# Attention into a long-convolution gate: batch 2 crossed by DMA, the last batch's complex sums on VectorE, a new order of all engines

## The chip, the cores and the metric

The kernel runs on one core of one Trainium2 chip. The metric is device time of that core in microseconds, the median of several runs. The engines have their usual names: TensorE (PE, with its weight loads as PEld), VectorE (DVE), ScalarE (ACT), GpSimd (POOL) and SyncE (SP). POOL issues the loads that turn 32-bit inputs into 16-bit ones, SP the other transfers.

## The reference

Two operations follow each other. The first is attention with a bias that falls with distance, 4 batches, 8 heads, 768 positions, 64 columns a head. A query sees the first 8 keys and the 96 latest ones:

```
scores = q @ k^T / sqrt(64) - slope[h] * dist        # dist 96 for the far first keys
a = softmax(scores where (key < 8) or (0 <= query - key < 96))
x = (a @ v), heads side by side                      # [4, 768, 512]
```

The second takes x through a gated convolution over the whole sequence:

```
x1, x2, x3 = split(x @ w_proj)                       # 512 columns each
conv = irfft(rfft(x2) * rfft(filter))                # along the 768 positions
out = (x1 * conv * x3) @ w_out                       # [4, 768, 512], float32
```

## The kernel before, in words

**Stages of a batch.** Attention works on seven tiles of keys: each holds the 8 first keys and 120 further ones, so that one tile of keys and up to 216 queries cover the local window. The tiles form three groups c = 0, 1, 2 (tiles 0 and 1, 2 and 3, 4 to 6). For each pair of heads and each group PE forms the scores (`scores`, L759), ACT takes the exponential (L774), DVE multiplies by a mask that holds bias and window (L791; batch 0 adds the bias on PE instead, L753). For each half of the heads and each group, PE multiplies by the values (`values`, L809 and L814), DVE takes the reciprocal of the sum, and DVE or ACT normalises into `xn` (L833 on DVE as one instruction, L837 on ACT as one small instruction for each slice of 64 columns). PE turns `xn` (`transpose_x`, L854) and a copy puts it into `xT`.

From `xT` PE forms the gates x1 and x3 (`gate`, L932): ACT takes x1 out of PSUM with a scale (L318), and DVE multiplies x3 by it (L946). In the last batch ACT copies x3 too (L942) and DVE multiplies both in SBUF (L944).

The Fourier transform of 768 positions is split by butterflies (`butterfly`, DVE, L868 to L888) before the projection of x2 (`conv`, PE L993, copied into `ab`). Six spectral blocks X come out of one matmul each (`spectra`, L1124, copied into `X`). Blocks 0 and 1, and 2 and 3, are real and imaginary parts. Their complex product with the filter is four real products (DVE, L1142 and L1145 into `pp`) and a difference and a sum (DVE, L1153 and L1154). Blocks 4 and 5 have another form (L1131, L1134). In the last batch, which `SUMPE` names, the difference and the sum are left out: PE adds the four products while it transforms back, with six matmuls for each block of the output instead of four (L1023, L1027, L1030). DVE then joins the parts (`mixed`, L1088 to L1094), forms y (`gated`, L1108 and L1109), multiplies by the gates (L1113), and PE projects y by w_out (L1059). ACT or DVE scales the result into `ot`, and SP stores it (L1070).

**Turning queries and keys.** The scores need queries and keys with the head's columns on the partitions, `QT` and `KT`. There are two ways. Batches 0 to 2 load them by head pairs, turn them on PE with an identity (`turned`, L707, L710), and copy them out of PSUM (one copy for a QT, three or four for a KT). Batch 3, which `TILES` and `CROSS` name, loads them by tiles of positions (`load_tiles`: 6 loads of queries, 7 of keys) and lets SP issue 13 transposing transfers from SBUF to SBUF through the crossbar (`cross`, L406). One such transfer writes 128 columns of all four head pairs in QT or KT. Two small transfers fill the 8 first keys into the other tiles (`kg` below, L392).

`qn` and `kn` (the loaded rows), `QT`, `KT`, `X` and `pp` exist once. So batch 3's loads overwrite the rows of batch 2, and its transposes overwrite the QT and KT of batch 2. The values and the gates have two buffers.

**What sets the order.** Every operation is a node of a graph (`Plan`), numbered as it is made. A long text, ORDER, lists the numbers in the order of issue, each with its engine and, for a group of matmuls, the PSUM banks that it takes: `83P0` is operation 83 on PE into bank 0. A copy out of PSUM may stand on A (ACT) or V (DVE). Each engine runs its own operations in the order of the text, and waits are put in where data demand them. `i1b5` stands for one spare matmul of 512 columns into bank 5, which computes nothing. Since SP's queue is one sequence, a transfer that waits holds all behind it. The same holds for POOL.

The order before puts batch 2's transposes on PE between the last projections and spectra of batch 0, and its scores behind them. Batch 3's crossing stands behind the last of POOL's loads.

Of the kernel before, what the change touches and what calls it, by code (L numbers as in the profile page):

```python
# [17 lines left out]
P = 128  # L18
# [10 lines left out]
def act(n):  # L29
    return 0.06 + n / 1200.0  # L30
# [11 lines left out]
0V 1V 2A 3G 45S 30A 47S 4V 34V 6A 9A 32G 56S 49S 5V i1b5 22P0 55G 23A 54G 7G 24A 10V 17P1 8V 33V 25V 51G 18A  # L42
35G 19A 12P2 13A 46V 52G 37A 48V i2b5 83P0 38A 53G 81P3 72G 20V 26A 61G 63G 21A 14V 44V 50V 15V 39V 201P1 93P2
36V 87P4 84A 202V 57V 60G 43A 82A 207V 95P3 16A 94A 97P67 209V 85P2 65G 64G 29V 11V 62G 88A 41V 91P0 203V 66G
96V 149P45 239G 42A 236G 86V 98A 204A 234G 150A 40V 89P3 121P67 151P45 238G 58V 208V 90V 205V 122A 152A 117P23
92V 99P67 206V 103P45 211V 233G 212V 118A 213V 235G 100A 119P23 101P67 153P01 104A 105P45 120A 102A 154A 27V
214V 115P23 237G 106V 215V 59S 116A 107V 155P67 78A 216V 110P01 111V 128P23 232G 157P45 156A 77A 217V 67G
220P6 112V 162P01 221A 158V 108P6 73A 113P7 129V 130V 123P23 109A 224P6 159V 131P4 114V 79A 222P7 245G 68G
341P5 241G 243G 225A 163V 124V 76A 223A 218P6 31V 240G 164V 125V 337P0 132V 28V 339P1 244G 340V 165P7 126P4
127V 247G 160P2 74A 335P1 338A 137P4 342A 166V 193V 139A 161V 133P7 376P23 219A 242G 336V 246G 354P45 414P01  # L50
377A 138P6 69G 167P2 355A 134P3 415A 183V 135A 184V 351P45 352A 192V 194V 140V 373P01 186V 185V 136V 343P6
374A 459G 169A 248G 195V 172P7 70G 71G 171P4 464G 187V 196V 173A 226P01 347P2 227A 345P3 411P45 251G 344V 252G
353V 349P0 145P6 75A 174V 249S 412A 348V 141P2 346V 254G 357P45 350V 228A 417P01 147A 375V 253G 420P67 188V
168P3 255G 197V 458G 256G 470G 356V 189V 143A 170V 142P2 465G 418A 471G 144V 175P0 358A 146P1 421A 382P67 198V
191V 460G 360P23 177A 413V 199V 148V 80A 190V 383A 379P45 380A 258P0 463G 361A 259A 229P67 416V 200V 378V
271P1 363P45 272A 230A 422V 275P2 461G 364V 273P3 231A 250S 466G 276A 284P6 419V 385P01 362V 274A 384V 286P7
359V 260P2 386V 365V 387V 462G 560P3 287A 479G 478G 285A 469G 261A 368P45 381V 279P0 366P1 472G 561A 473G 369V
468G 277P2 288V 423P67 370V 280A 262P3 289V 264P0 278A 367A 371P1 424V 263A 467G 425V 372A 282V 566P2 428P45
266P1 390P67 257G 265A 706G 567A 562P0 281V 267A 429V 388P3 391V 563A 179P2 430V 564P1 392V 176P4 181A 180P0
565A 389A 269V 576P67 268V 182V 178V 426P1 577A 431P2 393P0 432V 427A 394V 579P45 687G 580A 598P67 639P23 640A  # L60
396P0 698G 572P1 574P4 270V 395P5 298P2 407P3 696G 573A 599A 474G 397A 450V 570P1 568P6 449V 451V 695G 452V
404P5 575A 299A 408P7 694G 409A 403P4 571V 684G 398V 636P23 585P01 453V 410V 690G 569A 283V 454V 405A 600V
637A 582P67 445P4 480G 586A 481G 699S 399P2 447A 406V 433P3 446P4 455V 477G 702G 292P5 583A 435A 401A 456V
457V 645P67 607P01 448V 693G 293A 300P3 638V 646A 290P2 294P5 441P4 295A 304P6 442P5 581V 476S 608A 482G 584V
443A 400P7 475S 578V 302P4 697G 296P0 609V 688G 301A 291A 647V 303A 444V 689G 402V 485P1 604P45 297A 305A 587V
642P23 486A 307V 306V 605A 601P67 641V 691G 643A 685S 483P0 496P1 593P23 602A 308V 594V 603V 497A 484A 498P4
606V 588P67 487P5 589V 683G 701G 499A 595A 437P4 309V 489P0 590V 490A 488A 704G 310V 615P67 439A 692G 644V
311V 703G 610P23 611V 616V 700S 653P01 491P5 617A 438P4 612V 312V 511P2 440V 654V 686S 434P3 313V 596P4 618P6
512A 597A 492A 619A 500P7 655V 591P2 592A 613P5 314V 493V 501A 502P4 509P6 494V 648P01 504P7 656P2 705G 614A
624P5 510A 787S 649V 505A 513V 657A 632P6 503A 436V 315V 620P7 507V 629P4 621P3 626A 323P5 495V 506V 789S 514V  # L70
625P2 650A 508V 785S 634A 622A 651P0 324A 652A 628P6 784S 515P7 786S 517P5 529P1 518A 623V 527P3 627V 316V
675V 523P0 516A 528A 519P2 630A 670P5 525P3 793S 526A 521P7 633P6 530A 520A 791S 332P3 674V 317P2 524A 635V
333A 631V 672A 662P3 522A 803P45 790S 677V 806P67 800P01 318A 664A 801A 788S 676V 326P2 804A 795S 532V 327A
329P3 320P0 678V 330A 321A 796S 707P2 679V 663P3 807A 797P01 531V 680V 794S 825P67 533V 708A 534V 822P45 798A
682V 826A 720P2 666P0 535V 805V 536V 665V 671P3 823A 537V 681V 828P67 673V 721A 819P45 711P1 658P3 668A 820A
712A 799V 792S 829A 724P2 861P01 827V 870P67 660A 867P45 725A 722P3 540V 538V 802V 319S 334S 871A 733P2 868A
539V 723A 709P6 809P45 726P3 541V 734A 808V 554P7 331S 872V 810V 727A 735P3 542P2 830V 811V 862A 863V 555A
710A 814P01 836P45 864P67 736A 815V 543A 824V 837V 667P3 816V 865A 659P2 869V 838A 866V 715P6 713P7 661V
878P01 325S 669V 714A 548P2 728P7 812P3 879V 716A 821V 880V 737V 817P6 831P45 729A 873P01 839P7 322S 832V 730V
818A 813A 874V 551P3 731V 833A 875V 328S 732V 718V 557P6 881P4 738V 834P5 876P0 545P1 840A 835A 882A 877A  # L80
856P7 556S 717V 841P4 904V 741P0 903V 719V 745P5 546A 749P1 558A 742A 843A 549A 746A 857P6 842P0 906V 905V
907V 908V 851P2 858A 909V 750A 753P7 559S 844A 747P5 754A 739P4 743P1 751P0 883P7 744A 912P1 748A 910V 740A
852P4 752A 756V 859A 755V 913A 924P6 853A 936P2 552A 925A 911V 884P5 757V 854A 938P6 914P3 845V 937A 758V
916P2 939A 915A 860V 928P3 759V 888P6 210A 917A 760V 553S 940V 761V 929A 920P4 550S 918P3 886A 919A 926P2 941V
764V 921A 923V 922V 932P3 889P5 927A 898P4 933A 930P3 544S 894P2 885A 946P7 931A 762V 896A 942P3 935V 957P1
846P2 934V 855V 947A 958A 961P7 943A 944P1 962A 948P3 945A 763V 959P0 949A 963P7 960A 964A 765V 951V 950V
847P1 781P0 547S 891A 965V 966V 952V 967V 769P5 899P7 848A 953V 770A 900A 968V 954V 969V 772P2 955V 970V 956V
766P3 849A 773A 971V 850V 974V 774S 901A 972V 893P2 767A 782A 975V 775P7 973V 890A 892V 778P3 771S 895A 897V
982P2 768S 985V 779A 902V 783S 976P3 887V 776A 979P7 986V 983A 987V 993P2 989P6 988V 780S 994P 1001P0 980V
# [1208 lines left out]
```

## Time and profile before

| | |
|---|---|
| median of three runs | 165.75 us (165.38 to 165.85) |
| span of the profiled execution | 163.0 us, first to last instruction |
| instructions | 4256 |
| granted TensorE clock | 0.999 |
| POOL's last load issued | 82.6 to 84.4 us |
| last crossing issued (end of the issue) | 100.8 us |

The profiled execution has no time of its own beside its span. The median of the runs stands 2.75 us above that span, and this difference is taken as what lies around the span. The views give busy times for each engine, a table of stretches of time, groups of instructions by source line and shape, waits by what ended them, and packets by DMA queue (q0 holds what POOL issues, q1 what SP issues). In a group's row stand the line, engine, operation, output and inputs with shapes, the count, then the busy time in us and the mean duration in ns, and the idle time of the engine just before.

### The profile page before, as it was taken

How to read it: one execution, taken by the hardware profiler on the slowest of the kernel's cores; microseconds unless marked ns; L12 is line 12 of the kernel's file. 1: busy time of each engine (PE TensorE's matmuls, PEld its weight loads, DVE VectorE, ACT ScalarE, POOL GpSimd, SP SyncE). 2: the span in 40 equal slices, each digit the busy share in tenths (PEclk: the TensorE clock that was granted, in tenths of full speed). 3: DMA queues.
4: the chain of work that ended last, by engine and by line, in shares of the span. 5: the costliest groups of instructions: out<-in, count | busy, mean ns of one | idle time of the engine just before them, and what ended most of it. 6: DMA issues, size and time to landing. Idle time of an engine off the chain costs nothing.

```text
span 163.0 us, 4256 instructions
## 1 busy us (share of the span) xinstructions
PE 154.0 (94%) x1604; PEld 94.7 (58%) x1604; DVE 151.6 (93%) x356; ACT 150.3 (92%) x327; POOL 76.8 (47%) x101
## 2 busy tenths in 40 slices
PE   6599997999999999999999999999999999999980
PEld 2274355866655777666577584445676664584440
DVE  6599699999999999999999999999999999999960
ACT  8999996999999999999999999999998999997850
POOL 7999199999979997999970000000000000000000
PEclk9999999999999999999999999999999999999999
DMA  5999999999999999999999964630100106000684
GB/s 170 200 166 164 165 150 138 147 158 174 190 162 154 139 136 136 149 153 163 161 129 162 134 121 101 236 150 0 64 4 6 66 0 253 5 4 0 264 332 178
DMA packets 84956, 21.95 MB, mean 135 GB/s; under 512 B 75584, under 2 KB 81992, under 8 KB 84936
## 3 DMA queue, kind: packets, MB, share of 16 engines
q0 software_dynamic: 73040, 12.11, 98.4%
q1 hardware_dynamic: 11896, 9.57, 21.4%
q8 instruction: 12, 0.20, 0.5%
q14 instruction: 8, 0.07, 0.1%
HBM read 25.40 MB, written 6.29 MB: 194 GB/s over the span
## 4 chain that ended last, share of the span: by engine, by line
PE 85%; ACT 9%; DVE 3%; issue 1%
PE bank L932 26%; PE bank L993 13%; PE bank L1059 13%; PE bank L759 7%; PE bank L854 4%; PE bank L809 4%; PE bank L707 3%; PE bank L1023 3%; PE bank L1124 3%; PE bank L814 3%; PE bank L753 2%; ACT E L774 2%; ACT KT L314 1%; PE bank L1030 1%; PE bank L690 1%; ACT QT L314 1%
## 5 line engine op out<-in xcount | busy, mean ns | idle before, releaser
L932 PE MATMUL bank<-xT,w 128*128 128x384 f16 x256 | 48.2, 326 | 0.0
L774 ACT ACTIVATE E<-bank 128x864 f16<-128x864 f32 x48 | 41.0, 911 | 0.3 <-PE bank L759 0.2
L932 PEld LDWEIGHTS <-w 128*128 128x128 f16 x256 | 23.9, 98 | 15.8 <-issue 0.3
L339 POOL DMA_DIRECT2D vn<-in_v_dram x28 | 26.3, 979 | 1.1 <-DMA w<-in_moe_w_proj_dram 1.1
L339 POOL DMA_DIRECT2D kn<-in_k_dram x25 | 21.8, 892 | 5.4 <-DMA vn<-in_v_dram 4.0
L1059 PE MATMUL bank<-wo,y 128*128 128x512 f16 (+1 forms) x100 | 22.6, 371 | 0.0
L339 POOL DMA_DIRECT2D qn<-in_q_dram x25 | 21.8, 885 | 0.1
L791 DVE TENSOR_TENSOR E<-E,mask 128x864 f16<-128x864 f16 x36 | 20.3, 591 | 0.0
L318 ACT ACTIVATE x<-bank 128x384 f16<-128x384 f32 x32 | 16.6, 547 | 0.0
L318 ACT ACTIVATE ot<-bank 128x512 f32<-128x512 f32 (+1 forms) x23 | 13.3, 610 | 3.5 <-PE bank L1059 3.1
L809 PE MATMUL bank<-vn,E 128*128 128x65 f16 x224 | 15.3, 193 | 0.9 <-DVE xn L833 0.7
L993 PE MATMUL bank<-w,xs 128*128 128x512 f16 x64 | 15.9, 379 | 0.0
L809 PEld LDWEIGHTS <-E 128*128 128x128 f16 x224 | 14.0, 97 | 2.3 <-DMA vn<-in_v_dram 0.4
L1059 PEld LDWEIGHTS <-y 128*128 128x128 f16 x100 | 9.5, 98 | 9.9 <-DVE y L1113 0.5
L814 PE MATMUL bank<-vn,E 128*128 128x65 f16 x192 | 15.0, 193 | 0.0
L314 ACT CAST eo<-bank 128x384 f16<-128x384 f32 x32 | 14.3, 513 | 0.6 <-PE bank L1030 0.2
L314 ACT CAST X<-bank 128x512 f16<-128x512 f32 x24 | 14.3, 636 | 0.4
L314 ACT CAST ab<-bank 128x512 f16<-128x512 f32 x24 | 14.3, 629 | 0.4 <-PE bank L993 0.3
L833 DVE TENSOR_TENSOR xn<-bank,rc 128x512 f16<-128x512 f32 (+1 forms) x19 | 14.3, 771 | 0.1
L814 PEld LDWEIGHTS <-E 128*128 128x128 f16 x192 | 13.1, 97 | 1.9 <-issue 1.2
L759 PE MATMUL bank<-QT,KT 64*128 64x216 f16 (+2 forms) x224 | 13.7, 242 | 0.0
L759 PEld LDWEIGHTS <-KT 64*128 64x128 f16 x224 | 7.9, 94 | 8.7 <-issue 6.8
(163 smaller groups left out, 334.1 us busy)
## 6 DMA issues: line engine op xcount, KB each, us to landing
out_dram<-ot SPq DMA_DIRECT2D x23, 256.0 KB
vn<-in_v_dram POOLq DMA_DIRECT2D x28, 120.0 KB, 7.6
kn<-in_k_dram POOLq DMA_DIRECT2D x16, 96.0 KB, 5.1
qn<-in_q_dram POOLq DMA_DIRECT2D x16, 96.0 KB, 5.2
w<-in_moe_w_proj_dram POOLq DMA_DIRECT2D x4, 256.0 KB, 5.8
kn<-in_k_dram POOLq DMA_DIRECT2D x7, 120.0 KB, 6.2
g<-in_moe_filter_fft_dram POOLq DMA_DIRECT2D x1, 768.0 KB, 10.6
qn<-in_q_dram POOLq DMA_DIRECT2D x6, 128.0 KB, 7.0
```

Of the source, the lines that this page charges most:

```text
L314: {"A": nc.scalar.copy, "V": nc.vector.tensor_copy, "G": nc.gpsimd.tensor_copy}[e](out, in_)
L318: self.nc.scalar.mul(out, in_, c)
L339: return self.g.op(eng, 0.57 + 0.00035 * nbytes[0] if eng == "G" else 0.5, lambda _: e.dma_start(dst, src), w=w, r=r, nbytes=nbytes, name= ...
L759: nc.tensor.matmul(bs[hh].f32()[:, off:off + w], self.KT[hs, hp, P * m:P * m + P], self.QT[hs, hp, KL * m:KL * m + w], start=(off == 0 and ...
L774: g.op("A", act(864), lambda _: nc.scalar.activation(eo, bs[0].two()[:, :, 0:432].rearrange("p h (m w) -> p h m w", m=2), Act.Exp, scale=s ...
L791: g.op("V", dve(864, 2), lambda _: nc.vector.tensor_mul(eo, eo, mk), r=[("mask", 2 * hp), ("mask", 2 * hp + 1)], w=[("E", hp, gi)], name=" ...
L809: nc.tensor.matmul(o[:, n, hh], ef[:, at:at + P], vt[:, t, 2 * hp + hh, 0:D + 1], start=first, stop=(t == 0), skip_group_check=True)
L814: nc.tensor.matmul(o[:, n, hh], ef[:, at:at + P], vt[:, t - 1, 2 * hp + hh, 0:D + 1], start=False, stop=True, skip_group_check=True)
L833: nc.vector.tensor_mul(to, o[:, :, :, 0:D], rc.to_broadcast([P, 2, 2 * nt, D]))
L932: nc.tensor.matmul(bk.f32()[:, 0:h], self.w[:, c, o + P * j:o + P * j + P], self.xT[:, c, h * s:h * s + h], start=(c == 0), stop=(c == 3))
L993: nc.tensor.matmul(bk.f32(), src[:, c], w[:, c, DM:2 * DM], start=(c == 0), stop=(c == 3))
L1059: nc.tensor.matmul(bk.f32()[:, 0:n], y[:, c, P * t:P * t + P], self.wo[:, c, cs], start=(c == 0), stop=(c == 3))
```

## The change

- `TILES` and `CROSS` name batch 2 as well: its 16 loads by head pairs become 13 loads by tiles, its 48 transposes on PE and the 16 copies out of PSUM go, and SP issues 13 crossbar transposes and two small copies for it.
- `SUMPE` is empty: in batch 3 DVE forms the difference and the sum (two instructions for each of two pairs of blocks), and PE's inverse has four matmuls for a block instead of six.
- `WHOLE` names batches 0 to 2: the products of blocks 0 to 3 are formed together, in two instructions of 2048 columns instead of four of 1024, and their sums in two of 1024 instead of four of 512. `parts` places them behind all four X.
- ORDER is new throughout. Beside the order it moves some operations between ACT and DVE. Of normalising, ACT gets 8 of 24 (5 before); of the QT copies 1 of 8 (6 of 12); of the KT copies 5 of 8 (7 of 12). Two of the filter's copies and one `ab` go from ACT to DVE. Batch 2's first scores come directly behind the last turning of batch 1's `xn`, and batch 3's scores earlier among the projections of batch 2. The spare matmuls are one at the start and two ahead of the last output projection.
- The further options (`PAIR_T`, `PAIR_AB`, `PAIR_X`, `PAIR_EO`, `PAIR_OT`) join two banks into one copy; all are empty, so their paths aren't taken. `ab` and `ot` become views of one tile each.

```diff
 ORDER = """
-0V 1V 2A 3G 45S 30A 47S 4V 34V 6A 9A 32G 56S 49S 5V i1b5 22P0 55G 23A 54G 7G 24A 10V 17P1 8V 33V 25V 51G 18A
...
-990P 777S 977A 978S 997P7 998P 995A 984S 991A 999A 1002P 1003V 981S 996S 992S 1000S 1004S
+45S 34V 1V 2A 0V i1b2 4V 3G 5V 22P4 23A 47S 8V 56S 11V 49S 32G 53G 46V 6A 17P1 52G 7G 18A 24V 25V 12P0 13A 26A 19V
...
+979P 980A 981S 982P6 983P 984V 985S i2b0 986P4 987P 988V 989S
 """
...
-    SUMPE = (3,)
+    SUMPE = ()
...
+    WHOLE = (0,1,2)
...
-    TILES = (3,)
-    CROSS = (3,)
+    TILES = (2, 3)
+    CROSS = (2, 3)
...
+    def parts(self, b):
+        self.spectra(b, (2, 3))
+        if b in self.WHOLE:
+            self.products(b, (0, 1, 2, 3))
+        self.spectra(b, (4, 5))
...
+    def products(self, b, pair):
+        nc, g, X, DM = self.nc, self.g, self.X, self.DM
+        n, m = pair[0] // 2, len(pair) // 2
+        xs = X[:, pair[0]:pair[0] + 2 * m]
...
+        two = lambda x: x.rearrange("p (k c) n -> p k c n", c=2)
+        for to, h, key in ((p1, self.h1, "p1"), (p2, self.h2, "p2")):
+            g.op("V", dve(1024 * m, 2), lambda _, to=to, h=h: nc.vector.tensor_mul(
+                two(to), two(xs), h[:, n:n + m, None].to_broadcast([P, m, 2, DM])),
...
         def sums(_):
-            nc.vector.tensor_sub(xs[:, 0], p1[:, 0], p2[:, 1])
-            nc.vector.tensor_add(xs[:, 1], p1[:, 1], p2[:, 0])
+            x, y, z = two(xs), two(p1), two(p2)
+            nc.vector.tensor_sub(x[:, :, 0], y[:, :, 0], z[:, :, 1])
+            nc.vector.tensor_add(x[:, :, 1], y[:, :, 1], z[:, :, 0])
```

More of the change, by code (lines that the diff above doesn't have):

```diff
@@ L47 @@
[L47 to L61, printed above, removed]
@@ L146, in op @@
             b.left += 1
+            p.add(b.owner)
+            if "P" not in cost:
+                p.update(x for x in b.users if "P" in x.cost)
             b.users.append(o)
-            p.add(b.owner)
         o.preds = p
@@ L985, in conv @@
         X, y, w = self.X, self.y, self.w
-        for i in range(2):
-            for t, (src, key) in enumerate((
-                    (self.xo[:, i], ("xo",)), (self.xs[:, 3 * i], ("xe", "xd")), (self.xs[:, 2 - i], ("xe", "xd")))):
-                bk = g.bank()
+        units = [(i, t, src, key) for i in range(2) for t, (src, key) in enumerate((
+            (self.xo[:, i], ("xo",)), (self.xs[:, 3 * i], ("xe", "xd")), (self.xs[:, 2 - i], ("xe", "xd"))))]
+        pair = b in self.PAIR_AB
+        for u in range(0, 6, 1 + pair):
+            bks = [g.bank() for _ in range(1 + pair)]
+            for bk, (i, t, src, key) in zip(bks, units[u:]):
                 def proj(_, src=src, bk=bk):
```

204 lines of the change are left out of this document (128 added, 76 removed).

## The prediction

> **What bounds the kernel now.** I read the page's busy times first, then the table of stretches.
>
> ```profile
> span 163.0 us, 4256 instructions
> PE 154.0 (94%) x1604; PEld 94.7 (58%) x1604; DVE 151.6 (93%) x356; ACT 150.3 (92%) x327; POOL 76.8 (47%) x101
> ...
> 20.00:30.00 10.00, 8.86 (x150) 5.66 (x151) 9.90 (x24) 8.26 (x13) 10.00 (x13) 1.00 2.13 143
> 140.00:150.00 10.00, 10.00 (x90) 6.60 (x88) 9.99 (x23) 8.52 (x20) 0.00 (x0) 1.00 0.01 2
> 150.00:163.00 13.00, 8.51 (x45) 4.02 (x42) 7.38 (x22) 6.37 (x13) 0.00 (x0) 0.99 0.64 243
> ```
>
> A row gives the stretch and its length, then busy time of PE, weight loads, DVE, ACT and POOL, clock, DMA share and GB/s. Between these rows, from 30 to 120 us, all three engines are at 9.8 or more of each 10, and the averages don't say which binds. Busy time counts the overlap of neighbours, so I need the pace of each:
>
> ```profile
> 15.18 7.40 ACT L774 ACTIVATE E<-bank 128x864 f16<-128x864 f32 x9
> ...
> 154.08 0.62 DVE L944 TENSOR_TENSOR g<-g,x 128x384 f16<-128x384 f16 x2
> ...
> 30.30 0.34 PE bank L707 x6
> ...
> L774 ACT ACTIVATE E<-bank 128x864 f16<-128x864 f32 x48 | 41.0, 911 | 0.3 <-PE bank L759 0.2
> L944 DVE TENSOR_TENSOR g<-g,x 128x384 f16<-128x384 f16 x8 | 2.6, 348 | 0.0
> ```
>
> Nine exponentials of 911 ns end in 7.40 us: each after the first adds 0.81, its duration less 0.10. On DVE the second product adds 0.27, its duration less about 0.07. A transpose on PE costs 0.34/6 = 0.056. At these paces DVE's instructions still come to about 151 us, ACT's and PE's to about 145. DVE has the least slack: it idles some 7 us before its end, nearly all at the two ends:
>
> ```profile
> DVE y L500 <- ACT y L498: 1.8, 1, 1.8
> DVE ot L320 <- PE bank L1059: 1.5, 1, 1.5
> DVE pp L639 <- DMA g<-in_moe_filter_fft_dram: 1.3, 1, 1.3
> ```
>
> So the change is worth what it takes from DVE, as long as no new wait reaches DVE.
>
> **The change, part by part.** The letter after each number of the order gives the engine; I counted them by kind of operation in both orders.
>
> *PE.* Batch 2 loses 48 transposes (8 tiles by 6): 48 x 0.056 = -2.7. Batch 3's inverse loses 16 matmuls of 128 columns, taken at the same pace: -0.9. Together -3.6, off the bound. Of three spare start-up matmuls one stays, and two go ahead of the last output projection (see the tail).
>
> *Evacuations and normalising.* The copies out of those transposes go, and others change hands:
>
> ```profile
> L314 DVE COPY QT<-bank 128x768 f16<-128x768 f16 x6 | 4.1, 686 | 0.3 <-PE bank L710 0.2
> L314 DVE COPY KT<-bank 128x720 f16<-128x720 f16 x5 | 3.4, 671 | 0.0
> L314 DVE COPY KT<-bank 128x120 f16<-128x120 f16 x5 | 1.2, 233 | 0.0
> L833 DVE TENSOR_TENSOR xn<-bank,rc 128x512 f16<-128x512 f32 x12 | 8.0, 673 | 0.0
> L833 DVE TENSOR_TENSOR xn<-bank,rc 128x768 f16<-128x768 f32 x7 | 6.6, 940 | 0.0
> L320 DVE TENSOR_SCALAR ot<-bank 128x512 f32<-128x512 f32 x1 | 0.7, 681 | 0.0
> L314 ACT COPY QT<-bank 128x768 f16<-128x768 f16 x6 | 5.2, 867 | 0.0
> L314 ACT COPY KT<-bank 128x720 f16<-128x720 f16 x7 | 5.6, 799 | 0.0
> L837 ACT ACTIVATE xn<-bank,rc 128x64 f16<-128x64 f32 x44 | 9.8, 407 | 0.0
> ```
>
> On DVE: QT copies go from 6 to 7, +0.6; KT copies from 5 to 3, each 0.671 + 0.233 less 0.14 and a third smaller one taken at 0.1, -1.7; normalising from 19 to 16 (one of 512, two of 768), -2.3; one ab and two filter copies arrive, priced by the ot row as 128x512 from PSUM, +1.8; small moves (a cast, clearings, table steps, one xT copy), none above 0.7, counted the same way, -0.8. Sum -2.4. On ACT: QT from 6 to 1, -3.8; KT from 7 to 5, at about 1.1 with its small copies, -2.2; normalising from 44 to 76 slices at 9.8/44 = 0.22, +7.1; the rest -1.3. Sum -0.2: ACT gains nothing, as what the crossbar spares it goes into normalising that DVE gives up.
>
> *Products.*
>
> ```profile
> L1142 DVE TENSOR_TENSOR pp<-X,h 128x1024 f16<-128x1024 f16 x8 | 5.4, 677 | 0.0
> L1153 DVE TENSOR_TENSOR X<-pp 128x512 f16<-128x512 f16 x6 | 2.5, 414 | 0.0
> L1113 DVE TENSOR_TENSOR y<-y,g 128x1536 f16<-128x1536 f16 x6 | 5.5, 949 | 0.0
> ```
>
> 512, 1024 and 1536 columns take 414, 677 and 949: about 267 per 512 and 147 fixed, of which 77 is left at DVE's pace. Batches 0 to 2 merge eight instructions into four: 12 x 0.077 = -0.9. Batch 3 gains four additions of 512, 4 x 0.345 = +1.4. Together +0.5. The merged products wait for four X instead of two; the order puts gate products, masks and butterflies of the next batch ahead of them, and without that cover each batch would cost one more ACT copy, about 0.5. Batch 3's odd inverses now wait for the second sums; before DVE needs them stand three gate products (0.348 each) and one of 949, 1.7 us at pace, against three inverses and one ACT copy, about 1.3. I cost it at nothing; uncovered, at 1.3.
>
> **DVE in all: -2.4 + 0.5 = -1.9.**
>
> *Start.* DVE's work ahead of the first filter sum grows by 1.7 us by my count, and the filter is issued 0.7 earlier, so the wait of 1.3 on it closes. But DVE's first cast now stands ahead of the table steps and may idle for its load. Between -1.3 and +1.0; I take -0.6.
>
> *Tail.*
>
> ```profile
> 155.87 0.56 DVE L1113 TENSOR_TENSOR y<-y,g 128x768 f16<-128x768 f16 x1
> ...
> 158.55 0.42 DVE L320 TENSOR_SCALAR ot<-bank 128x256 f32<-128x256 f32 x1 [1.52 <-PE bank L1059]
> ```
>
> PE has some 1.7 us of output projections left after the last y*g; afterwards 2.4, the two spare matmuls of 0.21 among them. I take +0.4 (0 to +0.7).
>
> *The crossing of batch 2.* POOL issues 13 loads for 16, in about the same time. SP gets 13 transposes and two small key copies, behind two copies into batch 1's values, and ahead of those of batch 2, all of batch 3's crossing and the first stores. POOL's loads of batch 3 overwrite the crossed tiles, so POOL waits on each crossing, and behind it batch 3's values and keys wait.
>
> ```profile
> 77.28 1.55 SPq L406 DMA_TRANSPOSE QT<-qn  x1
> ...
> 84.49 2.50 SPq L406 DMA_TRANSPOSE QT<-qn  x2
> ...
> 46.44 0.97 PE bank L993 x4
> 60.58 0.29 PE bank L759 x4
> ...
> 60.69 1.02 DVE L946 TENSOR_TENSOR g<-bank,x 128x384 f16<-128x384 f32 x2
> ...
> POOL kn L339 <- DMA vn<-in_v_dram: 4.0, 1, 4.0
> ...
> kn<-in_k_dram POOLq DMA_DIRECT2D x7, 96.0 KB, 4.9
> ```
>
> Batch 1's scores free KT and QT. In PE's new order they end 2.1 us of work behind where the first L993 stands now (46.44): 48.5. The fifth tile's load is issued at about 47 (42.6 us of POOL's work ahead, its wait of 4.0 on top) and lands 4.9 later, at 52. Two transposes take SP 2.50, so 1.25 each: q1 at 48.5, the fifth, with the small copy among them, issued by 55.5. Batch 2's first scores stand 1.2 us of PE work earlier than now (60.58): 59.4. DVE's work ahead of their first mask is 1.1 us longer than ahead of the row at 60.69: DVE needs the exponential at 61.8 and so the scores at about 60.5. The landing decides:
>
> ```profile
> q0 software_dynamic: 1770, 0.21, 135.1%
> q1 hardware_dynamic: 491, 0.13, 65.3%
> ...
> q0 software_dynamic: 3822, 0.45, 240.0%
> ...
> q1 hardware_dynamic: 4176, 1.01, 107.7%
> ...
> q0 software_dynamic: 13845, 1.70, 225.1%
> ```
>
> These are packets by queue in 80 to 83 (two rows), 85 to 88, 88 to 96 and 48 to 60 us; q0 holds POOL's loads. A crossing is 512 packets. The one issued at 77.28 moved in 80 to 83, with loads beside it: 3 us to start, 3.1 to move. In 85 to 88 the loads ran at 1274 a us and no crossing moved, though one had been issued at 84.49. In 88 to 96, loads ending, eight crossings took 8 us. In 48 to 60 the loads run at 1154 a us, near full. So five crossings are ready at 48.5 + 3 + 5 x 1.0, but not before the last issue plus 3: 58.5; or, at 3.1 each, at 67. No wait, or 6.5 us. A crossing that stands alone can't show what a queue of them gets, so I lean to the row of 88 to 96, take 1.9 each and get 61: 0.5 of DVE's time.
>
> A rule of the Trainium skill speaks to this. DMA: Bandwidth & Descriptors, SWDGE vs HWDGE vs iDMA, says that each DMA engine takes turns between the internal queues that software and hardware feed. By that rule a queued crossing always moves, there is no wait, and the sum is 0.5 lower. The trace agrees in 80 to 83 only; its row of 85 to 88 speaks against it.
>
> **The sum.** 163.0 - 1.9 - 0.6 + 0.4 + 0.5 = 161.4 us of span. The median of the runs, 165.75, stands 2.75 above the profiled span: 164.1 us.
>
> **The rivals.**
> - *The crossing of batch 2 comes late (slower).* At 2.5 each it lands at 64: DVE waits 3.5 instead of 0.5, 167.1; at 3.1, 170.1. It decides from a wait of 2.2 us on. For it: 85 to 88, and loads near full in 48 to 60; POOL blocking on the crossings helps only once its backlog, some five us by the landing time, is through. Against it: the crossing of 80 to 83 did get through beside the loads.
> - *The crossing hides whole.* No wait: 163.6, and 162.5 if the start gains its full 1.3 and the tail costs nothing. For it: 88 to 96.
> - *Batch 3 is late.* Batch 2's 13 x 512 = 6656 packets delay batch 3's loads by 6656/1274 = 5 us if each costs as much as a loaded one, or by 20 at the row of 80 to 83, where 491 stood against 3 x 1154 - 1770 loads not moved, 3.4 each. Batch 3's last scores stand 3.7 us of PE work earlier than now, but its crossing, which now starts in earnest at 84.49, can start once batch 2's scores are through, near 72. By that I reckon 10 us of cover; a delay of 13 would show 3: 167.
> - *Nothing comes of it.* DVE's relief goes into waits inside the denser order, as PE and ACT have little slack either: 165.7.
>
> **How the numbers follow.** Forecast 0.42 (own range 163.0 to 165.7, the ends of start and tail), hidden whole 0.13, crossing late 0.29, batch 3 late 0.08, nothing 0.08. A measurement here can tell 0.3%, 0.5 us. Faster: 0.42 + 0.13 = 0.55; same 0.08; slower 0.29 + 0.08 = 0.37. The range for 8 in 10 leaves out the best starts below and waits beyond 5.4 us above: 162.3 to 169.0.
>
> **What would show it.** The crossing right: no wait of PE L759 on DMA KT or QT above 1 us near 60, SP's first transpose near 48, DVE at 9.9 in each ten us from 20 to 150. Wrong: PE and DVE dip together between 58 and 72, and POOL waits for qn and kn there. The counts: no L1027 rows, L707 at 66 transposes, L833 at 16, L837 at 76, products of 2048 columns near 1.2 us; busy times of DVE near 149.7, ACT near 150, PE near 150. The start: L639 without its wait on the filter. The forecast falls if a wait of over 2 us reaches DVE anywhere between 20 and 150, whichever step it comes from, or if ACT, which loses nothing, turns out to be the bound.

## The result, and the profile after

The change makes the kernel slower: 179.08 us (median of four runs, 177.65 to 179.62) against 165.67 us, a ratio of 1.083 (95% interval 1.076 to 1.089). The profiled execution took 177.65 us, its span is 175.9 us, 12.9 us more than before. The forecast was 164.1 us.

The page after, its first lines and four rows in 40 slices of 4.4 us (a digit is the busy share in tenths, GB/s what the DMA engines moved):

```profile
span 175.9 us, 4173 instructions
PE 156.7 (89%) x1540; PEld 93.6 (53%) x1540; DVE 151.4 (86%) x344; ACT 150.5 (86%) x344; POOL 75.4 (43%) x98
...
PE   6698939999999936987599999999999999999991
...
DVE  4999929999999972679299999999999999999952
...
DMA  5999999999999999999999999447000040102764
GB/s 186 181 160 184 151 161 146 149 174 181 153 164 126 161 134 149 155 146 105 133 152 144 138 164 137 109 132 239 6 0 7 0 177 6 60 34 89 283 257 175
```

DVE and ACT are as busy as before (151.4 against 151.6, 150.5 against 150.3). So the loss isn't work but idle time, and it lies in holes that PE and DVE share. The table of stretches after gives their sizes (PE, weight loads, DVE, ACT, POOL, clock, DMA share, GB/s):

```profile
20.00:30.00 10.00, 6.69 (x93) 3.99 (x89) 6.46 (x14) 6.23 (x10) 9.45 (x13) 0.83 2.18 153
60.00:70.00 10.00, 5.39 (x55) 3.50 (x51) 5.43 (x9) 4.97 (x10) 5.48 (x7) 0.84 1.87 145
70.00:80.00 10.00, 9.37 (x83) 6.03 (x83) 7.48 (x13) 7.85 (x17) 3.68 (x4) 0.82 1.66 148
80.00:90.00 10.00, 7.06 (x71) 3.73 (x69) 6.65 (x15) 7.41 (x12) 4.52 (x5) 1.00 2.36 126
```

Three holes: at the start, in 60 to 80 us, and in 80 to 90 us. DVE lacks 14 us in these four rows. PE's granted clock is 0.82 to 0.84 in three of these rows and full in the fourth. The waits after (total, times, longest, in us) and three transfers out of the chain that ended last (start, duration) say what the holes waited for:

```profile
POOL qn L347 <- DMA vn<-in_v_dram: 10.1, 5, 2.9
PE bank L767 <- DMA QT<-qn: 5.2, 2, 4.6
PE bank L817 <- DMA vn<-vn: 3.2, 1, 3.2
PEld L767 <- DMA KT<-kn: 3.2, 1, 3.2
```

```profile
18.84 6.03 DMA vn<-vn
59.21 8.37 DMA QT<-qn
74.45 11.06 DMA KT<-kn
```

(Lines after are 8 higher than before around here: the scores are L767.) The first hole is the small copy of the first values; the second is a crossing of queries that was issued at 59.21 and complete 8.4 us later; the third is batch 2's last crossing of keys, complete 11.1 us after its issue, at 85.5. In the kernel before no wait of PE on a transfer is above 0.4 us.

One more pair of rows has to be set side by side. First the DMA row and the GB/s row of the page before, which the prediction did not use:

```profile
DMA  5999999999999999999999964630100106000684
GB/s 170 200 166 164 165 150 138 147 158 174 190 162 154 139 136 136 149 153 163 161 129 162 134 121 101 236 150 0 64 4 6 66 0 253 5 4 0 264 332 178
```

The DMA engines were busy without a break up to about 95 us already before, and they are so up to about 110 us after. The view of the DMA queues gives what was moved until the crossings were done, before (0 to 104 us) and then after (0 to 118 us):

```profile
DMA packets 81636, 16.10 MB, mean 155 GB/s; under 512 B 75215, under 2 KB 81367, under 8 KB 81622
```

```profile
DMA packets 89605, 17.86 MB, mean 151 GB/s; under 512 B 83167, under 2 KB 89335, under 8 KB 89591
```

The rate is nearly the same, 3% lower, and the amount is 1.76 MB larger: for the most part 13 crossings of 0.13 MB. At 151 GB/s that is 11.7 us, an estimate of what the added bytes cost.

### The profile page after: what moved, and what is told of

The parts are those of the page before. It is cut to its first block, busy times and chain, and to the rows that moved or that the text cites. A ratio compares the mean times of both kernels' runs of the same rounds, so it can differ in the third digit from the quotient of the medians.

```text
span 175.9 us, 4173 instructions
## 1 busy us (share of the span) xinstructions
PE 156.7 (89%) x1540; PEld 93.6 (53%) x1540; DVE 151.4 (86%) x344; ACT 150.5 (86%) x344; POOL 75.4 (43%) x98
## 4 chain that ended last, share of the span: by engine, by line
PE 69%; DMA 16%; ACT 8%; SPq 3%; DVE 2%; issue 1%; DVEq 0%
PE bank L942 21%; PE bank L1100 12%; PE bank L1007 11%; DMA KT<-kn 6%; PE bank L767 6%; DMA QT<-qn 5%; PE bank L817 4%; PE bank L862 4%; DMA vn<-vn 3%; PE bank L1172 3%; PE bank L822 3%; SPq L414 3%; PE bank L1038 2%; ACT E L782 2%; DMA h<-in_k_dram 2%; PE bank L715 2%
## 5 line engine op out<-in xcount | busy, mean ns | idle before, releaser
L782 ACT ACTIVATE E<-bank 128x864 f16<-128x864 f32 x48 | 42.5, 976 | 11.1 <-PE bank L767 10.9
L942 PE MATMUL bank<-xT,w 128*128 128x384 f16 x256 | 51.0, 334 | 0.0
L347 POOL DMA_DIRECT2D qn<-in_q_dram x23 | 20.1, 885 | 10.9 <-DMA vn<-in_v_dram 10.1
L767 PE MATMUL bank<-QT,KT 64*128 64x216 f16 (+2 forms) x224 | 15.9, 257 | 8.2 <-DMA QT<-qn 5.2
L326 ACT ACTIVATE x<-bank 128x384 f16<-128x384 f32 x32 | 18.0, 602 | 2.3 <-PE bank L942 2.1
L767 PEld LDWEIGHTS <-KT 64*128 64x128 f16 x224 | 8.7, 98 | 19.5 <-issue 14.4
L326 ACT ACTIVATE ot<-bank 128x512 f32<-128x512 f32 (+1 forms) x23 | 15.3, 685 | 3.1 <-PE bank L1100 3.0
L817 PEld LDWEIGHTS <-E 128*128 128x128 f16 x224 | 14.5, 99 | 5.5 <-issue 3.8
L845 ACT ACTIVATE xn<-bank,rc 128x64 f16<-128x64 f32 x76 | 17.1, 514 | 0.0
L956 DVE TENSOR_TENSOR g<-bank,x 128x384 f16<-128x384 f32 x24 | 13.0, 543 | 4.6 <-PE bank L942 4.5
L322 ACT CAST X<-bank 128x512 f16<-128x512 f32 x24 | 15.8, 729 | 1.2 <-PE bank L1172 1.2
```

The source lines that it names most:

```text
L322: {"A": nc.scalar.copy, "V": nc.vector.tensor_copy, "G": nc.gpsimd.tensor_copy}[e](out, in_)
L326: self.nc.scalar.mul(out, in_, c)
L347: return self.g.op(eng, 0.57 + 0.00035 * nbytes[0] if eng == "G" else 0.5, lambda _: e.dma_start(dst, src), w=w, r=r, nbytes=nbytes, name= ...
L767: nc.tensor.matmul(bs[hh].f32()[:, off:off + w], self.KT[hs, hp, P * m:P * m + P], self.QT[hs, hp, KL * m:KL * m + w], start=(off == 0 and ...
L782: g.op("A", act(864), lambda _: nc.scalar.activation(eo, bs[0].two()[:, :, 0:432].rearrange("p h (m w) -> p h m w", m=2), Act.Exp, scale=s ...
L817: nc.tensor.matmul(o[:, n, hh], ef[:, at:at + P], vt[:, t, 2 * hp + hh, 0:D + 1], start=first, stop=(t == 0), skip_group_check=True)
```

## The experiments

Two theories stood at first. *Crossing*: batch 2's crossing shares the DMA engines with POOL's loads, and what comes out of them comes late. *Order*: the new order of the engines is slow by itself. Ratios are to the kernel before on the same chip, with 95% intervals.

| kernel | median us | ratio |
|---|---|---|
| e1_ones | 178.26 | 1.083 (1.074 to 1.092) |
| e2_pe2 | 175.61 | 1.067 (1.058 to 1.076) |
| e3_cross2_only | 185.80 | 1.126 (1.114 to 1.139) |
| e4_sums | 166.59 | 1.011 (1.003 to 1.020) |
| e6_crossing_first | 182.52 | 1.103 (1.097 to 1.110) |
| e7_pe2_ones | 170.56 | 1.036 (1.031 to 1.040) |
| e8_merge | 166.99 | 1.014 (1.010 to 1.018) |
| e9_spare_crossings | 177.46 | 1.076 (1.068 to 1.084) |
| e10_no_values | 176.37 | 1.073 (1.066 to 1.079) |
| e11_order_only | 171.47 | 1.042 (1.036 to 1.047) |
| e12_new_start | 167.41 | 1.018 (1.012 to 1.024) |
| e13_held_no_values | 170.76 | 1.039 (1.033 to 1.046) |
| e14_six_spare | 169.60 | 1.029 (1.022 to 1.037) |
| e15_late_spare | 173.56 | 1.050 (1.040 to 1.059) |
| e16_late_spread | 163.79 | 0.995 (0.992 to 0.998) |
| e17_order_of_before | 164.44 | 0.998 (0.995 to 1.001) |

The kernel before took 164.4 to 164.9 us beside them. e17 has the program text of the changed kernel with the settings and order of the one before, and shows that the experiments built so stand on the same ground:

> The program text of the changed kernel with the settings and the order of the kernel before, so the same instructions: the ground on which e3, e4, e8, e9 and e12 to e16 stand, and a look at whether the 0.9 us that e16 was under the kernel before come from the text or from the spare crossings. If from the text: 163.5 to 164.3. If the two are the same kernel: 164.3 to 165.3.

### The start: e1

```diff
-45S 34V 1V 2A 0V i1b2 4V 3G 5V ...
+45S 34V 1V 2A 0V 30A i1b2 4V 3G 5V ...
...
-103P01 209V 30V 105P67
+103P01 209V 105P67
```

> The changed kernel, with one step put back where it stood before: the memset of the ones of the first value tile (ones0) is on ACT again, right after its table step, not on DVE ahead of the filter sums. Theory 'start': the small copy vglob0 goes out near 11 us again, is done before PE's first values want it, and the hole in all engines at 20 to 30 us closes: 3 us less than the changed kernel, 175 to 177. Rival 'DMA paces': what is lost at the start is only waited for elsewhere, because batch 2's crossing ends when it ends: 178 to 180.

The start is mended: PE is at 9.87 and DVE at 9.53 in 20 to 30 us. Yet nothing is gained: against the kernel before on the same chip, both kernels stand at 1.083. The table of stretches of e1 shows where the rest went:

```profile
20.00:30.00 10.00, 9.87 (x163) 6.51 (x160) 9.53 (x21) 9.96 (x17) 10.00 (x13) 1.00 2.25 153
60.00:70.00 10.00, 5.99 (x40) 3.30 (x41) 4.79 (x7) 3.81 (x7) 5.05 (x6) 0.66 1.87 140
80.00:90.00 10.00, 6.45 (x42) 2.91 (x43) 3.17 (x7) 3.93 (x6) 4.71 (x6) 0.66 2.23 127
```

In 80 to 90 DVE now lacks 6.8 us, where it lacked 3.4. The engines came earlier to the same transfers and waited there. So the rival's range holds, and these rows fit its reason: the DMA engines set the pace here, and the hole ahead of that point cost next to nothing.

### The crossing alone, and the order without it: e3, e2, e7, e11

e3 is the kernel before with batch 2's crossing and nothing else of the change:

```diff
-    TILES = (3,)
-    CROSS = (3,)
+    TILES = (2, 3)
+    CROSS = (2, 3)
```

and in the order 13 tile loads in the places of the 16, b2's five late value loads ahead of wo, the crossings and key copies on SP behind wo, the PE turning left out.

> The kernel before, in its own order, with this one part of the change: batch 2 is loaded in 13 tiles and turned by the crossbar (13 crossings and two small copies on SP right behind the load of wo, the 16 loads replaced in their places, five value loads of batch 2 moved ahead of wo); the PE transposes and evacuations of batch 2 are gone, the sums stay on PE. Theory 'crossing': the crossings share the DMA engines with POOL's loads, batch 2's scores wait and batch 3's loads with them: 171 to 178. Rival 'order': the crossing hides in the order of before: 162 to 166.

It is slower by 21 us, beyond the range that was expected and worse than the whole change. The waits of PE in e3:

```profile
PE bank L766 <- DMA QT<-qn: 13.3, 3, 7.4
PE bank L766 <- DMA KT<-kn: 5.9, 1, 5.9
```

These 19 us are nearly all of the loss. So 'crossing' holds and does not need the new order; at the place that I gave it in the old one it costs even more.

The other way round, e2 and e7 keep the new order and turn batch 2 on PE again. In words for the numbers of the order:

```diff
-    TILES = (2, 3)
-    CROSS = (2, 3)
+    TILES = (3,)
+    CROSS = (3,)
 # ORDER, batch 2: the crossings and key copies on SP and the 13 tile loads out;
 # 16 loads by head pairs in the places of the 13;
 # over the 60 (e7: 70) steps ahead of the first scores, for each head pair:
+transposes of q on P, copy of q on A, transposes of k on P, copy of k on V (one on A)
 # e7 only: loads, turning and first scores by head pairs 0 1 2 3, ones0 as in e1
```

> The changed kernel, its order kept word for word where it can be, with batch 2's queries and keys loaded in 16 loads and turned by PE again (8 groups of transposes, 8 evacuations shared by DVE and ACT, put in over the 60 steps ahead of batch 2's first scores). Theory 'crossing': the holes at 60 to 90 us were the crossing's, so some 9 to 10 us go, less the 3 us that each of DVE and ACT has more to do: 170 to 173. Rival 'order': the new order is slow by itself, whoever turns batch 2: 177 to 183.

> e2_pe2 mended at two places that its trace shows: the ones on ACT early as in e1_ones, and batch 2's loads, turnings and first scores in the order of the head pairs 0 1 2 3, so that POOL does not wait for batch 1's turning. Theory 'bytes': without batch 2's crossing the start is worth what it seemed, both holes of e2_pe2 (20 to 30 and 50 to 75 us, 3.5 and some 4 us) close: 165.5 to 169. Rival 'order': the new order keeps losing somewhere: 171 to 176.

e2 lies between its two ranges. In its trace POOL waits 8.0 us at one place for batch 1's turning, and the start hole is still there. e7 mends both and gains 5.1 us over e2 (how much by each was not tried). But it, too, lies between its two ranges. It has 2.2 us more busy time on DVE than before and 3.6 more on ACT (turning is back), and DVE waits 3.6 us for the transposes that I put in. Most of its idle time lies where they stand: DVE is busy for 8.1 and 7.3 us of the ten in 50 to 60 and 60 to 70, and nearly full from 70 to 150. e11 takes the products apart again and puts the last batch's sums back on PE:

> e7_pe2_ones with the products of the pairs apart again and the sums of batch 3 on PE: of the change only the new order of the engines is left (with the ones early and batch 2's turning put in by hand). If the parts add up, the merge costs 2.3 us (e8_merge) and the sums 1.9 us (e4_sums), which leaves 170.6 - 4.2 = 166.4, within 165.5 to 167.5. Rival: the order was laid out for merged products and has no place for the parts; then nothing is won, 169.5 to 172.

171.47: the rival, nothing won; in the new order merge and sums do no harm. What is left of e7, 5.9 us over the kernel before, can't be divided between the order and the places that I gave the turning in it. 'Order' is therefore not refuted, but it is at most those 5.9 us.

### Sums and merge in the order of before: e4, e8

```diff
 # e4
-    SUMPE = (3,)
+    SUMPE = ()
 # e8
-    WHOLE = ()
+    WHOLE = (0,1,2)
```

> The kernel before, in its own order, with this one part of the change: the complex products of batch 3 are summed by DVE (two more pairs of sums, 0.68 us an instruction, and inverse transforms of 4 matmuls in place of 6). Theory 'crossing' gives this part about what the prediction gave it, 1.4 us more for DVE and as much less for PE: 165.5 to 167.5. Rival 'sums': in the last batch nothing covers them and each of the two pairs stands on the path: 168 to 170.

> The kernel before, in its own order, with this one part of the change: for batches 0 to 2 the products of the two pairs of spectra are made by one instruction each (2048 columns), the sums of both likewise; batch 3 and all turning as before. The prediction's term for it is 0.9 us less of DVE: 163.3 to 165.3 against 164.5 to 165.7 of the kernel before. Rival: the merged products wait for all four spectra and the inverse transforms for the whole of the sums, 1 to 2 us a batch on DVE: 166 to 169.

Both lose about 2 us. For e4 that was expected. For e8 it wasn't: it does take work from DVE, as these rows of its groups show,

```profile
L1201 DVE TENSOR_TENSOR pp<-X,h 128x2048 f16<-128x2048 f16 x6 | 7.1, 1218 | 0.0
L1209 DVE TENSOR_TENSOR X<-pp 128x1024 f16<-128x1024 f16 x3 | 2.1, 689 | 0.0
```

7.1 us for what 12 instructions of 677 took (8.1), and twice 2.1 for twice 2.5. That is 1.8 us less in these instructions, yet the kernel got 2.3 us slower, and DVE's busy time as a whole stayed (151.7 against 151.6). Two stretches of e8:

```profile
50.00:60.00 10.00, 10.00 (x156) 7.43 (x155) 8.93 (x18) 9.83 (x23) 10.00 (x13) 1.00 2.19 139
90.00:100.00 10.00, 9.57 (x86) 6.37 (x85) 9.49 (x15) 9.14 (x28) 0.00 (x0) 1.00 0.94 132
```

Before, DVE was at 9.97 and 10.00 here, PE at 10.00 in both. DVE now waits, and in the second stretch so do PE and ACT. Among the waits that e8 has and the kernel before has not are 1.6 us of ACT for PE's inverse transforms and 0.7 us of PE for the merged sums. So the merged work is waited for, as the rival said; which wait started each hole was not followed further.

### What a crossing costs the DMA engines: e5

A kernel of its own: loads alone, crossings alone, both at once.

```diff
+for n in range(13): load(a, n)              # POOL, 128 rows x 512, float32 to float16
+for n in reversed(range(13)): turn(t, n)    # SP, crossing
+(a copy on POOL that waits for the last crossing)
+for n in range(13): load(c, n)              # and at the same time
+for n in reversed(range(13)): turn(u, n)
```

> A kernel of its own that computes nothing of the reference: 13 loads by POOL's queue of 128 rows x 512 (float32 to float16, as batch 2's tiles), then 13 crossings of such tiles on SP's queue, then 13 loads and 13 crossings at the same time. Theory 'bytes': the DMA engines move about 145 GB/s (131 KB for a tile either way), whoever asks: 11 to 13 us for the loads, 12 to 14 us for the crossings, and the third stretch takes the sum of the two, 23 to 27 us. Rival 'mixing': side by side the two queues hinder each other and the third stretch takes over 30 us.

The queues of e5 in 8 to 12 us, loads alone, and in 48 to 52 us, both (q0 is POOL's queue, q1 SP's):

```profile
DMA packets 4668, 0.59 MB, mean 147 GB/s; under 512 B 4668, under 2 KB 4668, under 8 KB 4668
```

```profile
DMA packets 3665, 0.61 MB, mean 154 GB/s; under 512 B 3665, under 2 KB 3665, under 8 KB 3665
q0 software_dynamic: 2350, 0.30, 124.2%
q1 hardware_dynamic: 1315, 0.32, 63.2%
```

Its page, kinds of DMA issues with the median from issue to landing in the last column:

```profile
first<-in_k_dram POOLq DMA_DIRECT2D x6, 128.0 KB, 4.5
again<-in_q_dram POOLq DMA_DIRECT2D x6, 128.0 KB, 6.4
again<-in_k_dram POOLq DMA_DIRECT2D x6, 128.0 KB, 10.7
turned<-first SPq DMA_TRANSPOSE x13, 2.5
twice<-first SPq DMA_TRANSPOSE x13, 7.3
```

Side by side the two move 154 GB/s, hardly more than the loads alone (147), half of it for each. Both together took some 24 us, as 13 loads of 0.13 MB and 13 crossings of 0.13 MB do at 147. So 'bytes' holds for the third stretch, and 'mixing', at over 30 us, does not: the two share one rate, and at that rate a crossing's 0.13 MB are 0.9 us. Alone a crossing lands 2.5 us after its issue, beside loads 7.3.

The second stretch missed its 12 to 14 us. It took some 19, because SP issued a crossing only every 1.31 us and the DMA engines idled in between; each crossing moved in about 0.7 us, at some 215 GB/s. By these times the two kinds one after the other would need some 20 us. So up to about 2 us of what they took together, an estimate, may still be a loss by mixing.

### Loads out of the way: e6, e10, e13

e6 holds wo and batch 3's loads behind batch 2's last crossing:

```diff
-ldwo b3.ldq1 b3.ldk0 ...                (POOL, from 65 us on)
+b2.xbark5 | b3.ldk5 ldwo b3.ldq1 ...    (the first waits for the last crossing)
```

> e1_ones with the load of wo and all loads of batch 3 held on POOL's queue behind batch 2's last crossing (the first of them writes the tile that is crossed last), nothing else moved. Theory 'bytes': about 1 MB less is moved ahead of the end of the crossing, which ends near 78 us, not 85: the hole of all engines at 80 to 90 us closes, and the time is 171 to 175 if batch 3, whose loads then begin some 10 us later, still comes in time. Rival 'batch 3 or wo is late next': the same bytes are only waited for later, 177 to 186.

```profile
80.00:90.00 10.00, 9.98 (x125) 6.16 (x124) 10.00 (x23) 10.00 (x30) 8.74 (x11) 1.00 1.49 126
100.00:110.00 10.00, 2.03 (x14) 0.92 (x14) 4.00 (x7) 2.34 (x5) 0.00 (x0) 0.64 1.86 142
```

The hole at 80 to 90 is closed as the theory said, and a larger one has opened at 100 to 110, where batch 3's crossing is late: the rival's 177 to 186 holds. The same megabytes are waited for, at one place or the other.

e10 takes megabytes away instead, 14 value loads:

> e1_ones without the 14 value loads of batches 2 and 3 (those batches use whatever the value tiles hold; the small copies stay), about as much DMA time as the 13 crossings of batch 2 add. Theory 'DMA time': both holes of the changed kernel, at 60 and at 80 us, go with the loads though every crossing is still there: 165.5 to 170. Rival 'late crossing': batch 2's scores wait for the crossings as before: 175 to 179.

A miss: 176.37, within the rival's range. But its trace shows why it couldn't tell. POOL did not leave the gap empty; it issued wo at 56.75 (64.90 in the changed kernel) and began on batch 3 at 57.63, all beside batch 2's crossing. e13 joins e6's order and e10's missing loads:

> e10_no_values with the load of wo and batch 3's loads held behind batch 2's last crossing as in e6_crossing_first: from 50 to 70 us the DMA engines have batch 2's 13 tile loads and 13 crossings and nothing else, and what is loaded later is 7 value tiles less than in e6. (Left out: the value loads of batches 2 and 3.) Theory 'DMA time': the crossing ends near 66 us, the hole at 60 to 70 shrinks to some 2 us of DVE, that of e6 at 100 to 110 too: 165.5 to 170. Rival 'late crossing': a crossing lands some 8 us after its issue whatever is beside it, the first hole stays: 173 to 179.

```profile
60.00:70.00 10.00, 4.00 (x30) 2.24 (x31) 3.17 (x5) 3.17 (x6) 0.00 (x0) 0.66 1.37 140
70.00:80.00 10.00, 9.88 (x92) 6.38 (x91) 9.43 (x17) 9.78 (x20) 7.24 (x9) 1.00 0.99 110
80.00:90.00 10.00, 9.98 (x115) 5.77 (x113) 10.00 (x23) 10.00 (x31) 5.54 (x6) 1.00 2.48 153
```

170.76 lies between the two ranges, nearer to the theory's, and the rows say what each got right. The holes of e1 from 70 us on are gone, and 7.5 us with them: they went with the loads. The hole at 60 to 70 stays. It ends with the first scores of batch 2, which wait for this transfer of e13's chain:

```profile
56.48 9.38 DMA QT<-qn
```

A crossing still takes 9.4 us to land while batch 2's own loads run beside it. Not all of that is sharing: from 61.5 to 62.75 us, with this crossing still on its way, the DMA engines moved only 15 GB/s. So about 1 us of the 9.4, or more, is a delay of another kind. The changed kernel shows such a lull too (56.3 to 57.0 us, 36 GB/s); what it is stays open.

### The dose, and the place: e9, e14, e15, e16

These leave the kernel before whole and add crossings of the weight tile that nothing reads:

```diff
+for n in range(13):          # e14: 6, e16: 12
+    nc.sync.dma_start_transpose(y[:, :, P * (n % 6):P * (n % 6) + P], w[:, 0, 0:512])
 # e9, e14: on SP behind b1's small copies (44 us); e15, e16: into qn, from 101 us on
```

> The kernel before, whole and in its own order (batch 2 turned by PE), with 13 crossings more on SP's queue behind b1's second small copy: they turn columns of the weight tile into y, which nothing reads and batch 0 overwrites later, so no engine waits for them. Theory 'DMA time': the crossings take 13 times 0.9 to 1.3 us of the 16 DMA engines, and POOL's loads of batch 2, which are only just in time, land up to 12 us later: 171 to 177. Rival 'late crossing': what costs is only that scores wait for a crossing (its issue, its queue, its landing), so spare ones cost nothing: 164.5 to 167.

> e9_spare_crossings with 6 spare crossings in place of 13, at the same place: some 6 us of DMA time more in the stretch from 44 to 60 us. Theory 'DMA time' without slack: half of e9's loss, 169 to 172; with a slack of a few us in the loads of the kernel before, less than half: 165.5 to 169. Rival, that the loss of e9 came from something that 13 crossings do and 6 do not (SP's queue held for 20 us, small copies behind it): no loss, 164 to 165.5.

e9 costs 13.0 us (a little above its range), as much as the whole change, although no engine waits for a crossing. PE's waits in e9:

```profile
PE bank L715 <- DMA kn<-in_k_dram: 3.8, 2, 2.8
PE bank L715 <- DMA qn<-in_q_dram: 2.9, 2, 1.6
...
PE bank L817 <- DMA vn<-in_v_dram: 1.8, 2, 1.6
```

They are waits for POOL's loads, which come late instead. Six spare crossings cost 4.7 us: 0.79 MB, 5.2 us at 151 GB/s. By its interval e14 lost 3.6 to 6.1 us, so six crossings found between nothing and 1.6 us to spare; e9's 13 (1.70 MB, 11.3 us) found nothing. The loads of the kernel before had next to no reserve in this stretch.

> e9_spare_crossings with the same 13 spare crossings put behind batch 3's last crossing on SP's queue, near 104 us, where the DMA engines of the kernel before are at a tenth of their time (they turn the weight tile into the query tiles, which are done with). Theory 'DMA time': nothing waits for the DMA engines there, 164 to 166. Rival 'SP or ports': the crossings hinder the engines themselves or SP's stores wherever they stand, 168 to 177.

> e15_late_spare with its place mended: its trace shows that nothing waited for the DMA engines, but that the 13 spare crossings in a row held SP's queue for 17.8 us, batch 0's stores behind them, and ACT waited 8.8 us for an output tile. Here 12 spare crossings stand one behind each store of batches 0 and 1, from 101 us on, so that no store is held by more than one. Theory 'DMA time': a spare crossing costs nothing where the DMA engines are idle: 164 to 166. Rival 'ports': crossings slow the engines wherever they stand: 168 to 175.

e15 lost 8.7 us, but not to the DMA engines. A row of its SP queue (start, duration) and a wait of ACT:

```profile
102.75 17.83 SPq L1300 DMA_TRANSPOSE qn<-w  x13
```

```profile
ACT ot L327 <- DMA out_dram<-ot: 8.8, 1, 8.8
```

13 crossings in a row held SP for 17.8 us, batch 0's stores stood behind them, and ACT waited 8.8 us for an output tile. In e16 each crossing stands behind a store, and the loss is gone: twelve crossings from 101 us on cost nothing (163.79, at the lower edge of the runs of the kernel before; e17 is at 164.44). Thirteen transfers of the same kind cost 13 us at 44 to 60 us; twelve cost nothing where the DMA engines are mostly idle.

### The new start in the old order: e12

The first 200 steps of the order before, in the sequence and on the engines of the changed kernel.

> The kernel before with the first 200 steps of its order in the sequence and on the engines of the changed kernel (the ones early as in e1_ones), all later steps as before. The prediction's term for the start is 0.6 us less, between 1.3 less and 1.0 more: 163.3 to 165.7 against 164.7 of the kernel before. Rival: the join of the two orders costs more than the start gives: 166 to 168.

3.0 us slower, in the rival's range. The new start gives the old order nothing.

None of these edits makes a kernel that is faster than the one before by a mechanism that the runs show; what would explain the 0.5% of e16 was not found.

## Why the prediction was wrong, point by point

**What bounds the kernel.** Wrong by what it left out. The prediction took DVE, which idled least, as the bound and valued the change by what it takes from DVE. It read the DMA share only to price a landing, not as a resource with an end, although it had the row with it: 13845 packets in 48 to 60 us, "near full". e9 and e14 show what that row meant: transfers that no engine waits for cost 13.0 and 4.7 us, so up to there the DMA engines bound the kernel as well. That DVE had little slack is not refuted: e4 gives it 1.4 us more work and costs 2.1 (by its interval 0.4 to 3.3). That less work on DVE makes the kernel shorter was not shown by any run.

**PE, evacuations, products.** The counts came out as written. These groups of the kernel after give 66 transposes, 16 normalising instructions on DVE, 76 slices on ACT, products of 1.206 us:

```profile
L715 PE MATMUL bank<-ident,kn 128*128 128x128 f16 x36 | 3.4, 249 | 1.7 <-POOL ident masks.py:199 1.7
L715 PE MATMUL bank<-ident,qn 128*128 128x128 f16 x30 | 2.7, 238 | 0.0
...
L841 DVE TENSOR_TENSOR xn<-bank,rc 128x512 f16<-128x512 f32 x11 | 7.4, 675 | 0.1
L841 DVE TENSOR_TENSOR xn<-bank,rc 128x768 f16<-128x768 f32 x5 | 4.8, 954 | 0.1
```

The sum did too, as work: counts times mean durations over all groups of DVE are 177.0 us before and 174.9 after, -2.1 against -1.9. What did not come out is the sign that was named for it, DVE's busy time: 151.4, not 149.7. Busy time counts the overlap of neighbours once, and less of the work overlaps after. As time, merge (-0.9) and sums (+1.4) cost 2.3 and 2.1 us in the order of before (e8, e4). For the merge that does not test the prediction: its cover belongs to the new order, and there taking merge and sums back gained nothing (e11, 171.47 against e7's 170.56).

**The start.** L647 lost its wait on the filter, as written. The named risk came true (DVE's cast waits 1.2 us for its load), though DVE got more done in the first 10 us than before, 7.42 against 6.78. What cost 3.2 us was not named: the ones of the first value tile moved from ACT's start to a place behind the filter's first sum, and with them the small copy that reads them, issued at 18.84 instead of 10.83, where it met POOL's loads. Every moved step's waiters were to be followed; these were not. That it cost nothing in the end (e1, by its ratio) could not be known from the page.

**The tail.** From the end of the last y*g to the start of DVE's last instruction it grew from 2.1 to 2.8 us, +0.7 against +0.4 (0 to +0.7).

**From span to time.** The sum added 2.75 us, the distance of the median from the profiled span before. A profiled execution itself stands some 1.75 us above its span (177.65 and 175.9 after). So about 1 us of the 2.75 presumably came from a profiled execution that was faster than the median; it is small beside the loss.

**The crossing of batch 2.** This is the step that failed. The issue was right but for the start: in e1, without the start hole, SP issues the first transpose at 48.31 and the fifth tile's at 55.58 (forecast 48.5 and by 55.5); in the changed kernel both come some 3.5 us later, at 51.98 and 59.21. The price was too low at two places. First, the five were taken to be ready at 61, where the wait allowed for was 0.5 us, and the first scores ran at 64.0 in e1 (67.7 in the changed kernel): 8.4 us after the last issue against the 5.5 that 61 implies. By the prediction's own form, 48.3 + 3 + 5 x 2.5 is 64: not 1.9 us a crossing but the 2.5 of its first rival. Secondly, and larger, the sum had no term for what the crossing takes from the loads. "POOL issues 13 loads for 16, in about the same time" counted issues and not megabytes. The 1.76 MB are an estimated 11.7 us; the loss is 13.4. That the two lie so close may be luck in part: e7, without this crossing, still stands 5.9 us over the kernel before, and how the 13.4 divides between crossing and order stays open. That 13 crossings alone suffice for such a loss is shown in the old order (e9: 13.0).

**The rule that queues take turns.** The Trainium skill, DMA: Bandwidth & Descriptors, SWDGE vs HWDGE vs iDMA, says that an engine takes turns between software and hardware queues. e5 agrees: 2350 packets of the one queue and 1315 of the other in the same 4 us, neither held. What does not follow is that there is no wait. Taking turns gave each queue half of one rate, and the late one was whichever was needed first. The prediction's row of 85 to 88 us, in which no crossing moved, says little against the rule: the crossing issued at 84.49 had its first packets some 3.9 us later, at about 88.4. The one before had needed 3, and one alone in e5 needs 1.3. Why that takes longer beside loads stays open.

**The rivals.** "The crossing of batch 2 comes late" had the right place and the signs: PE and DVE dip together at 60 to 70. Its price ended at 170.1, since it stopped at the landing. "Batch 3 is late" had the mechanism, packets that delay loads; it reckoned 5 or 20 us of delay and took 10 us of cover, but looked for the delay only in batch 3. There the cover sufficed: in the changed kernel DVE is at 9.5 or more of each ten from 90 us to 150 and nothing waits long for batch 3; only in e6, where its loads are held back further, is it late. The delay fell on batch 2's own loads, its crossing and the values, ahead of 90 us. The range, up to 169.0, had no room for the bytes of all 13 crossings.

## What to carry to other kernels

Read the DMA row as an engine's row. Where it stood at 9 in every slice of this kernel, added transfers cost about their bytes at the rate that the row below shows, and whatever was wanted next paid, whether or not it waited for the added transfer. Before work is moved from an engine to DMA, add up the megabytes up to the point where the last load is wanted, and test the reserve with a few transfers that nobody reads. And a saving on the engine with the least idle time need not be one of the kernel if the merged work makes others wait: e8 took 1.8 us out of DVE's instructions and came out 2.3 us slower.

## What the hardware showed

- POOL's loads and SP's crossings together move no more than the loads alone (154 against 147 GB/s), in shares of about half; alone, crossings on SP's queue go out every 1.31 us (13 in 16.98) and land 2.5 us after their issue.
- Stores of larger packets are another matter: the four outputs of e5 left at 383 GB/s. The Trainium skill, DMA: Bandwidth & Descriptors, Specifications, gives 512 B as the least transfer for full rate. The loads and the stores fit this: all packets of the loads in e5 are under 512 B, those of the stores about 2 KB. But the stores also differ in direction and in having no cast, which no run here separates; and the crossings alone, under 512 B as well, were paced by SP's issues.
- A hole in the engines ahead of a point that the DMA engines paced cost next to nothing here: e1 removed 3.2 us of wait, and its ratio stayed at 1.083.
